# Routing kernel: the second products of 64-row pieces as two column halves side by side

## The chip, the cores and the metric

The kernel runs on one core of one Trainium2 chip. The metric is the device time of one execution in microseconds (us). TensorE does the matrix products, VectorE (DVE), ScalarE (ACT) and GpSimd (POOL) work on elements, SyncE (SP) issues transfers, and each engine works through its own queue in order. Matrix products read SBUF and write PSUM, which has eight banks of 512 float32 per partition here.

## The reference

A decayed linear attention over 8 batches, 8 heads, 576 positions and a head size of 64 gives 4608 rows of 512 values. A router then picks two of eight experts for every row, and each expert is a pair of products with a ReLU between them:

```
logits = x @ w_gate ; noisy = logits + log1p(exp(x @ w_noise)) * noise
top2 = the two largest of noisy ; weights = softmax over these two
for e in range(8):
    for k in range(2):
        mask = top2[:, k] == e
        h = maximum(x[mask] @ w1[e], 0)          # 512 -> 1024
        out[mask] += weight * (h @ w2[e])        # 1024 -> 512
```

## The kernel before

The first 195 us or so hold the attention, the routing and a few early expert tiles. After them the expert tiles follow one another.

**Pieces and tiles.** Each expert has room for 1216 rows: nine pieces of 128 rows and a tenth (number 9) of 64. `tiles()` puts one to four pieces into a tile and sorts the pieces of a tile by size, so a 64-row piece always comes first in its tile. Numbered in order, tiles 0 to 8 are early ones, and tiles 9 to 28 are the wide ones. The 64-row pieces lie in tile 9 (with three full pieces, expert 0), tile 11 (with one, expert 1), tile 13 (with two, expert 2), and tiles 16, 19, 22, 25 and 28 (with one each, experts 3 to 7). Before tiles 16, 19, 22, 25 and 28 lie two tiles of four full pieces each.

**The two products.** `wide()` (line 1050) makes the first product of tile i: for each of eight groups f, four matmuls (line 1063) of 128x128 weights against all the rows of the tile, so 128x512 for a tile of four pieces and 128x192 for a full piece and a 64-row one. The result takes a PSUM buffer `p`, and ACT or DVE applies the ReLU (lines 1046 and 1048) into `hT`, four SBUF buffers that each hold two groups. Between these matmuls lie those of the second product of tile i-1: `down()` (line 1081) cuts its 8 times m matmuls (m pieces) into eight parts of m. `second()` (line 1114) is one of them: 128 columns of `hT` as weights against a 128x512 slice of w2, eight of them accumulating into one PSUM buffer `po` per piece. For a 64-row piece the same 128 columns are loaded, and the lower 64 rows of the result are not used. The pieces come one after the other in the order of the tile.

**What follows a piece.** When the last of its eight matmuls is done, `finish()` (line 1134) reads `po`. Rows whose first choice is this expert are scaled on ACT or DVE (lines 1148 and 1150) and written by SP to a scratch array `yd`. For rows with their second choice here, DVE multiplies and adds the earlier half (line 1158), which POOL has gathered from `yd` (line 1129), and POOL scatters the sum into the output (line 1162). Of the 64-row pieces, the one of expert 0 goes the first way and the other seven go the second way. The second product of tile 28 has no next tile to lie in: it runs at the end, piece by piece, the 64-row piece first.

**Order.** The order of the work on each engine is laid down ahead by a planner (`Plan.run`). It knows an estimated cost for every operation, hands out buffers, and picks the operation that could start soonest. Buffers have quotas: the expert stream holds at most four PSUM buffers at a time while other streams are open, and `half` buffers (which hold `hT`, the gathered halves and the outputs) number 21. For a group, the planner sees one TensorE operation with all its matmuls. The gathers of the rows of later tiles (line 961) are paced: each waits for the last TensorE matmul that was emitted before it (`self.mm`). For a piece in which first and second choices meet, DVE prepares weights and indices from the gathered row (lines 1001 to 1007). In the last wide tile, POOL has a drain (line 1250) in its queue.

Of the kernel before, what the change touches and what calls it, by code (L numbers as in the profile page):

```python
# [21 lines left out]
F = 1024  # L22
DM = 512
KD = DM // P
KF = F // P
# [12 lines left out]
KEY = 8192.0  # L38
NOV = 64
HD = 64  # L40
C9 = 9
NU = 16
MID = 288.0
# [198 lines left out]
class Kernel:  # L242
# [42 lines left out]
    def setup(self):  # L285
# [764 lines left out]
    def wide(self, i, t, prio, g2=None):  # L1050

        pl, nc = self.pl, self.nc
        w, d = self.W[t[0]], self.t[i]
        n, xT, xv = d["w"], d["xT"], d["xv"]
        hT = d["hT"] = [pl.buf("half", "exp") for _ in range(4)]
        for f in range(KF):
            p = self.psum("exp")

            def pe(_, f=f, p=p):
                it = g2(f) if g2 else iter(())  # L1060
                for di in range(KD):
                    o = di * F + f * P
                    self.mm = nc.tensor.matmul(p.t[:, :n], lhsT=w.t[:, o:o + P], rhs=xv()[:, di, :n],  # L1063
                                               start=(di == 0), stop=(di == KD - 1))
                    next(it, None)
                for _ in it:
                    pass
            r, ww, c = [xT] + [(w, k) for k in range(KD)], [p], 0.435 * n / 256
            if g2:
                r2, w2, c2 = g2.deps(f)  # L1070
                r, ww, c = r + r2, ww + w2, c + c2
            pl.op("PE", c, pe, r=r, w=ww, prio=prio)
            hv = lambda f=f: hT[f // 2].t.bitcast(BF16).rearrange("p (f s) -> p f s", f=2)[:, f % 2, :n]
            op = pl.op({"ACT": 0.17 + 0.00084 * n, "DVE": 0.1 + 0.00115 * n}, 0, lambda g, p=p, hv=hv: self.relu(
                g, hv(), p.t[:, :n]), r=[p], w=[(hT[f // 2], f)], prio=prio)
            if g2:
                for s in g2.ends(f):
                    self.finish(i - 1, g2.t, s, prio)
        return op

    def down(self, i, t):

        nc = self.nc
        e, js, _ = t
        w, d = self.W[e], self.t[i]
        po = d["po"] = [self.psum("exp") for _ in js]
        hT, m = d["hT"], len(js)
        part = lambda g: [divmod(x, KF) for x in range(g * m, g * m + m)]

        class Down:  # L1090
            def __call__(_, g):
                for s, f in part(g):
                    self.second(e, po[s], hT, self.off(js)[s], f)
                    yield

            @staticmethod
            def deps(g):
                return ([(hT[f // (KF // len(hT))], f if len(hT) == 4 else f // 2) for s, f in part(g)] +
                        [(w, KD + f // 2) for s, f in part(g)], [po[s] for s in sorted({s for s, f in part(g)})],
                        0.216 * m)  # L1100

            @staticmethod
            def ends(g):
                return [s for s, f in part(g) if f == KF - 1]
        Down.t = t
        return Down()

    def second(self, e, po, hT, c, f):


        k = KF // len(hT)
        hv = hT[f // k].t.bitcast(BF16).rearrange("p (f s) -> p f s", f=k)[:, f % k]
        o = KD * F + f * DM
        self.mm = self.nc.tensor.matmul(po.t, lhsT=hv[:, c:c + P], rhs=self.W[e].t[:, o:o + DM],  # L1114
                                        start=(f == 0), stop=(f == KF - 1))

    def prev(self, i, t, prio):
        pl, nc = self.pl, self.nc
# [15 lines left out]
    def finish(self, i, t, s, prio):  # L1134
        pl, nc, tc = self.pl, self.nc, self.tc
        e, js, _ = t
        d = self.t[i]
        j = js[s]
        k = self.kind(e, j)
        g, io, _, src = d["gi"][s]  # L1140
        src = list(src) if isinstance(src, tuple) else [src]
        po, n = d["po"][s], self.size(j)
        if k != "S":
            y = pl.buf("half", "exp")

            def ev(eng, y=y, po=po, g=g, n=n):
                if eng == "ACT":
                    nc.scalar.activation(y.t[:n], po.t[:n], Act.Copy, scale=g()[:n])  # L1148
                else:
                    nc.vector.tensor_scalar(y.t[:n], po.t[:n], g()[:n], None, Alu.mult)  # L1150
            pl.op({"ACT": 0.69, "DVE": 0.7}, 0, ev, r=[po] + src, w=[y], prio=prio)
            r0 = P + YOFF[e] + j * P
            key = self.ydk.setdefault(e, pl.fix())
            pl.op("SP", 0.07, lambda q, y=y, r0=r0, n=n: nc.sync.dma_start(
                out=self.yd[r0:r0 + n, :], in_=y.t[:n]), r=[y], w=[(key, j)], prio=prio, dma=0.7)
        if k != "F":
            o, b = pl.buf("half", "exp"), d["prv"][s]
            pl.op("DVE", 0.75, lambda _, o=o, b=b, po=po, g=g, n=n: nc.vector.scalar_tensor_tensor(  # L1158
                o.t[:n], po.t[:n], g()[:n], b.t[:n], Alu.mult, Alu.add), r=[po, b] + src, w=[o], prio=prio)

            def scat(_, o=o, io=io, n=n):
                ins = nc.gpsimd.indirect_dma_start(  # L1162
                    out=self.out[:, :], out_offset=IOff(ap=io()[:n], axis=0), in_=o.t[:n, :], in_offset=None,
                    bounds_check=N - 1, oob_is_err=False).ins
# [7 lines left out]
    def record(self):  # L1172
        pl = self.pl
# [7 lines left out]
        for u in range(NU + 1):  # L1181
# [14 lines left out]
            if u and u % 4 == 0:  # L1196
                pr = u - 0.4
# [5 lines left out]
        ts = self.tiles()  # L1203
# [3 lines left out]
        last = {t[0]: i for i, t in enumerate(ts)}  # L1207
# [7 lines left out]
        for i, t in enumerate(ts[:ne]):  # L1215
            pr = 100 + 4 * i
            while fetched < min(ne, i + 3):
                self.fetch(fetched, ts[fetched], 100 + 4 * fetched)
                fetched += 1
            begun = [self.up(i, t, pr)]  # L1220
            g = self.down(i, t)
            for k in range(KF):
                r, w, c = g.deps(k)
                pl.op("PE", c, lambda _, g=g, k=k: [0 for _ in g(k)], r=r, w=w, prio=pr)
                for s in g.ends(k):
                    self.finish(i, t, s, pr)
        prev = None
        for i in range(ne, len(ts) + 1):
            pr = 100 + 4 * i
            while fetched < min(len(ts), i + 1 + ahead):  # L1230
                self.fetch(fetched, ts[fetched], 100 + 4 * fetched - 2)
                fetched += 1
            if i < len(ts):
                e = ts[i][0]
                if i == last[e] and e + 3 < E:
                    self.weights(e + 3, pr, False, begun)
                late = i > ne and ts[i - 1][0] < e and any(self.kind(*x) != "S" for x in self.pieces(ts[i - 1]))
                if not late:
                    self.prev(i, ts[i], pr)
                begun = [self.wide(i, ts[i], pr, prev)]  # L1240
                if late:
                    self.prev(i, ts[i], pr)
            else:
                e, po, hT = ts[-1][0], self.t[i - 1]["po"], self.t[i - 1]["hT"]
                for s in range(len(po)):
                    pl.op("PE", 1.74, lambda _, s=s: [self.second(e, po[s], hT, self.off(ts[-1][1])[s], f) for f in range(KF)],
                          r=[(hT[f // 2], f) for f in range(KF)] + [(self.W[e], KD + f) for f in range(4)], w=[po[s]], prio=pr)
                    self.finish(i - 1, ts[-1], s, pr)
            if i == len(ts) - 1:
                pl.op("POOL", 6.0, lambda _: self.nc.gpsimd.drain(), prio=pr - 6, after=self.scats[i - 2][:1])  # L1250
            if i < len(ts):
                prev = self.down(i, ts[i])
# [159 lines left out]
```

## Time and profile before

| | |
|---|---|
| median of 3 runs | 440.3 us (438.19 to 440.85) |
| profiled execution | 441.0 us, span 439.4 us |
| TensorE busy | 385.7 us (88%) |
| GpSimd busy | 286.3 us (65%) |
| ScalarE busy | 240.0 us (55%) |
| VectorE busy | 179.7 us (41%) |
| mean DMA rate | 240 GB/s |

Line numbers (L1114) are those of the kernel. `PE` is TensorE's matmul row, `PEld` its weight loads. A matmul's record is longer than the distance to the next one, as they are pipelined: what a stream of them takes is read from start to start. Idle time of an engine is put down to what ended it. A few matmul records are missing from a trace.

### The profile page before, as it was taken

To read this page: it belongs to the slowest core of one execution; us is meant where nothing else is said; L and a number is where in the kernel's file an instruction comes from. 1 tells how busy PE (TensorE), PEld (TensorE's weight loads), DVE (VectorE), ACT (ScalarE), POOL (GpSimd) and SP (SyncE) were. 2 spreads that over 40 slices of the span, in tenths; PEclk is the share of its full clock that TensorE was granted. 3 is DMA by queue.
4 is the path that set the end of the run, shared out by engine and by line. 5 is a ranking of instruction groups with operands and counts; after the bars stand their busy time and mean duration, and the time that the engine had idled before them with its cause. 6 is when DMAs were issued, how large, how long until landed. Compare 5 with 4: busy or idle time off the path is not lost. (4 is left out here: it accounts for less than half of the span.)

```text
span 439.4 us, 11080 instructions
## 1 busy us (share of the span) xinstructions
PE 385.7 (88%) x4252; PEld 245.4 (56%) x4288; DVE 179.7 (41%) x489; ACT 240.0 (55%) x398; POOL 286.3 (65%) x355
## 2 busy tenths in 40 slices
PE   1787884889898959899979999999999999999992
PEld 1665774777676746575545545555454454454451
DVE  2544388778378278213043334026025031131221
ACT  3589693866787436466554747446536524424320
POOL 8875678997789337553446566566577677567344
PEclk9999597969899969999999999999999999999998
DMA  7999999999999988448399897895799997645323
GB/s 193 276 309 233 291 240 310 318 212 247 314 263 196 227 168 242 118 137 297 116 325 387 261 382 236 276 383 167 251 352 278 292 212 224 187 157 174 121 78 140
DMA packets 102489, 105.34 MB, mean 240 GB/s; under 512 B 31870, under 2 KB 80511, under 8 KB 102434
## 3 DMA queue, kind: packets, MB, share of 16 engines
q1 hardware_dynamic: 87170, 67.72, 51.3%
q0 software_dynamic: 15264, 36.89, 32.7%
q8 instruction: 34, 0.56, 0.5%
q14 instruction: 21, 0.17, 0.1%
HBM read 83.20 MB, written 26.63 MB: 250 GB/s over the span
## 5 line engine op out<-in xcount | busy, mean ns | idle before, releaser
L1114 PE MATMUL ps<-W,half 128*128 128x512 bf16 x608 | 202.8, 383 | 0.7 <-issue 0.2
L1063 PE MATMUL ps<-big,W 128*128 128x512 bf16 (+4 forms) x636 | 189.0, 330 | 4.0 <-DVE half L1048 2.8
L1046 ACT ACTIVATE half<-ps 128x512 bf16<-128x512 f32 (+5 forms) x179 | 90.2, 506 | 117.6 <-PE ps L1063 100.7
L961 POOL DMA_INDIRECT xg<-xd,xi x80 | 83.1, 1039 | 64.6 <-ACT half L1046 20.5
L1114 PEld LDWEIGHTS <-half 128*128 128x128 bf16 x640 | 62.6, 99 | 72.6 <-issue 5.6
L1063 PEld LDWEIGHTS <-W 128*128 128x128 bf16 x640 | 63.0, 98 | 47.6 <-issue 0.3
L1158 DVE SCALAR_TENSOR_TENSOR half<-ps,xg,half 128x512 f32<-128x512 f32 (+1 forms) x39 | 29.2, 749 | 79.9 <-PE ps L1114 68.6
L1162 POOL DMA_INDIRECT out_dram<-half,xg x39 | 38.8, 995 | 26.3 <-issue 12.5
L515 DVE TENSOR_TENSOR half<-ps,mask 128x512 bf16<-128x512 f32 x64 | 40.0, 683 | 20.2 <-PE ps L507 20.0
L1129 POOL DMA_INDIRECT half<-yd,xg x39 | 39.4, 1011 | 11.9 <-issue 10.4
L276 ACT ACTIVATE half<-ps 128x1024 bf16<-128x1024 bf16 (+1 forms) x33 | 32.7, 1010 | 12.1 <-PE ps L482 9.4
L482 PE MATMUL ps<-ident__69,half 128*128 128x128 bf16 x256 | 23.8, 251 | 16.6 <-ACT half L449 9.1
L457 POOL TENSOR_TENSOR half<-big,tab 128x1024 bf16<-128x1024 f32 x15 | 28.6, 1904 | 10.3 <-DMA big<-in_q_dram 10.3
L1037 PE MATMUL ps<-half,W 128*128 128x256 bf16 (+1 forms) x288 | 29.8, 260 | 4.5 <-ACT half L276 2.8
L464 POOL TENSOR_TENSOR half<-big,tab 128x512 bf16<-128x512 f32 x32 | 33.0, 1046 | 0.0
L1148 ACT ACTIVATE half<-ps,xg 128x512 f32<-128x512 f32 (+1 forms) x32 | 21.8, 685 | 16.1 <-PE ps L1114 15.8
L482 PEld LDWEIGHTS <-half 128*128 128x128 bf16 x256 | 18.6, 114 | 19.5 <-ACT half L449 9.6
L1037 PEld LDWEIGHTS <-W 128*128 128x128 bf16 x288 | 24.6, 100 | 8.2 <-issue 3.8
L276 ACT ACTIVATE tb<-ps 64x512 bf16<-64x512 f32 x32 | 18.9, 590 | 13.5 <-PE ps L540 13.3
L276 ACT ACTIVATE W<-big 128x1024 bf16<-128x1024 f32 x21 | 21.4, 1055 | 5.7 <-DMA big<-in_moe_w_dram 5.5
L276 ACT ACTIVATE xT<-ps 128x512 bf16<-128x512 f32 (+1 forms) x40 | 19.9, 556 | 7.2 <-PE ps L656 5.0
L1158 DVE SCALAR_TENSOR_TENSOR half<-ps,gm,half 128x512 f32<-128x512 f32 x6 | 4.5, 751 | 46.9 <-ACT half L1148 39.8
(170 smaller groups left out, 415.7 us busy)
## 6 DMA issues: line engine op xcount, KB each, us to landing
big<-in_moe_w_dram SPq DMA_DIRECT2D x40, 512.0 KB, 8.9
yd<-half SPq DMA_DIRECT2D x41, 256.0 KB, 5.2
big<-in_k_dram SPq DMA_DIRECT2D x32, 256.0 KB, 6.1
big<-in_q_dram SPq DMA_DIRECT2D x16, 512.0 KB, 6.0
big<-in_v_dram SPq DMA_DIRECT2D x32, 256.0 KB, 6.3
W<-in_moe_w_dram POOLq DMA_DIRECT2D x12, 512.0 KB, 10.5
xd<-xg SPq DMA_DIRECT2D x16, 264.0 KB, 5.0
xg<-xd,xi POOLq DMA_INDIRECT x80, 4.4
```

What stands on the lines that cost most here:

```text
L276: self.nc.scalar.activation(out, in_, Act.Copy)
L464: self.eng(e).tensor_tensor(o, i, t, Alu.mult)
L482: nc.tensor.transpose(v[:, hp, x, :], i[:, y, hp * P:(hp + 1) * P], ident.t)
L515: nc.vector.tensor_tensor(S.t.bitcast(BF16).rearrange("p (h c x) -> p h c x", h=2, c=2)[:, h], p[h].t.rearrange("p (c x) -> p c x", c=2), ...
L961: ins = nc.gpsimd.indirect_dma_start(out=x.t[:n, :], out_offset=None, in_=self.xd[:rows, :], in_offset=IOff(ap=xi.t[:n, h:h + 1], axis=0), ...
L1037: nc.tensor.matmul(pv()[:, f2, :], lhsT=w.t[:, o:o + P], rhs=xv()[:, di, :n], start=(di == 0), stop=(di == KD - 1))
L1046: self.nc.scalar.activation(o, i, Act.Relu)
L1063: self.mm = nc.tensor.matmul(p.t[:, :n], lhsT=w.t[:, o:o + P], rhs=xv()[:, di, :n], start=(di == 0), stop=(di == KD - 1))
L1114: self.mm = self.nc.tensor.matmul(po.t, lhsT=hv[:, c:c + P], rhs=self.W[e].t[:, o:o + DM], start=(f == 0), stop=(f == KF - 1))
L1129: pl.op("POOL", 1.3, lambda _, b=b, iy=iy, n=self.size(j): nc.gpsimd.indirect_dma_start(out=b.t[:n, :], out_offset=None, in_=self.yd[:rows ...
L1158: pl.op("DVE", 0.75, lambda _, o=o, b=b, po=po, g=g, n=n: nc.vector.scalar_tensor_tensor(o.t[:n], po.t[:n], g()[:n], b.t[:n], Alu.mult, Al ...
L1162: ins = nc.gpsimd.indirect_dma_start(out=self.out[:, :], out_offset=IOff(ap=io()[:n], axis=0), in_=o.t[:n, :], in_offset=None, bounds_chec ...
```

## The change

For a 64-row piece, the eight matmuls of the second product become sixteen. Each has 64 columns of `hT` as weights against 256 of the 512 columns of w2: the left half of the result goes to partitions 0 to 63 of the piece's PSUM buffer, the right half to partitions 64 to 127, both in its first 256 elements. So two matmuls with the same weights stand next to each other on the two column halves of the array.

These sixteen no longer lie between the matmuls of the next tile's first product. The eight parts of `down()` are now made of the full pieces only (n of them), and the 64-row piece follows in one block behind the last part. `deps` and `ends` are told so, and the planner's cost of the last part grows by 1.05. In the last tile the 64-row piece stays first, with a cost of 0.95 in place of 1.74.

`finish()` reads such a piece in two instructions of 64x256, one for each half, in place of one of 64x512; the planner's costs for them become 0.86 on ACT and for the multiply-add on DVE, and 0.8 for the scaling on DVE.

```
@@ down
-        part = lambda g: [divmod(x, KF) for x in range(g * m, g * m + m)]
+        full = [s for s in range(m) if self.size(js[s]) == P]
+        short = [s for s in range(m) if self.size(js[s]) < P]
+        n = len(full)
+        part = lambda g: [(full[x // KF], x % KF) for x in range(g * n, g * n + n)]
+        alone = lambda g: [(s, f) for s in short for f in range(KF)] if g == KF - 1 else []
...
+            def rest(g):
+                for s in short if g == KF - 1 else ():
+                    self.halves(e, po[s], hT, self.off(js)[s])
...
+    def halves(self, e, po, hT, c):
+        k = KF // len(hT)
+        for f in range(KF):
+            hv = hT[f // k].t.bitcast(BF16).rearrange("p (f s) -> p f s", f=k)[:, f % k]
+            o = KD * F + f * DM
+            for y in range(2):
+                self.mm = self.nc.tensor.matmul(po.t[y * HD:(y + 1) * HD, :MIDC], lhsT=hv[:, c:c + HD],
+                                                rhs=self.W[e].t[:, o + y * MIDC:o + (y + 1) * MIDC],
+                                                start=(f == 0), stop=(f == KF - 1), skip_group_check=True)
+
+    @staticmethod
+    def sums(po, n):
+        return [(slice(0, DM), po.t[:n])] if n == P else [
+            (slice(y * MIDC, (y + 1) * MIDC), po.t[y * HD:(y + 1) * HD, :MIDC]) for y in range(2)]
@@ wide, behind the last matmul of a group
+                if g2:
+                    g2.rest(f)
@@ finish
-            pl.op("DVE", 0.75, lambda _, o=o, b=b, po=po, g=g, n=n: nc.vector.scalar_tensor_tensor(
-                o.t[:n], po.t[:n], g()[:n], b.t[:n], Alu.mult, Alu.add), r=[po, b] + src, w=[o], prio=prio)
+            pl.op("DVE", 0.75 if n == P else 0.86, lambda _, o=o, b=b, po=po, g=g, n=n: [nc.vector.scalar_tensor_tensor(
+                o.t[:n, c], x, g()[:n], b.t[:n, c], Alu.mult, Alu.add) for c, x in self.sums(po, n)],
+                r=[po, b] + src, w=[o], prio=prio)
```

More of the change, by code (lines that the diff above doesn't have):

```diff
@@ L40 @@
 HD = 64
+MIDC = DM // 2
 C9 = 9
@@ L1223, in record @@
                 r, w, c = g.deps(k)
-                pl.op("PE", c, lambda _, g=g, k=k: [0 for _ in g(k)], r=r, w=w, prio=pr)
+                pl.op("PE", c, lambda _, g=g, k=k: ([0 for _ in g(k)], g.rest(k)), r=r, w=w, prio=pr)
                 for s in g.ends(k):
@@ L1245, in record, with last @@
                 for s in range(len(po)):
-                    pl.op("PE", 1.74, lambda _, s=s: [self.second(e, po[s], hT, self.off(ts[-1][1])[s], f) for f in range(KF)],
+                    def last(_, s=s):
+                        c = self.off(ts[-1][1])[s]
+                        if self.size(ts[-1][1][s]) < P:
+                            self.halves(e, po[s], hT, c)
+                        else:
+                            for f in range(KF):
+                                self.second(e, po[s], hT, c, f)
+                    pl.op("PE", 1.74 if self.size(ts[-1][1][s]) == P else 0.95, last,
                           r=[(hT[f // 2], f) for f in range(KF)] + [(self.W[e], KD + f) for f in range(4)], w=[po[s]], prio=pr)
```

21 lines of the change are left out of this document (12 added, 9 removed).

## Prediction

> **What bounds the kernel now.** I read the page first, then the stretches, then TensorE's waits, then the end.
>
> ```profile
> span 439.4 us, 11080 instructions
> PE 385.7 (88%) x4252; PEld 245.4 (56%) x4288; DVE 179.7 (41%) x489; ACT 240.0 (55%) x398; POOL 286.3 (65%) x355
> ...
> PE   1787884889898959899979999999999999999992
> ```
>
> TensorE is filled from about the middle on, and all the second products of 64-row pieces lie there. The busy time of each engine by stretch, and then all of TensorE's waits behind 195 us, say how full it is:
>
> ```profile
> 234.00:413.00 179.00, 177.95 (x985) 91.44 (x1004) 50.79 (x84) 88.31 (x154) 117.38 (x116) 1.00 0.82 257
> 413.00:440.00 27.00, 18.50 (x104) 9.69 (x104) 6.00 (x8) 5.04 (x12) 10.86 (x11) 0.94 0.28 99
> ...
> PE ps L1063 <- DVE half L1048: 2.8, 1, 2.8
> PE ps L983 <- DMA xg<-xd,xi: 0.6, 1, 0.6
> ```
>
> The columns are span, PE, PEld, DVE, ACT, POOL, granted clock, DMA share, GB/s. From 234 to 413 us TensorE is busy 177.95 of 179.00 us at full clock. The waits are two, both before 234 us. So a matmul less in this stretch is its whole time less, as long as nothing else gets late.
>
> The one large wait stands at 224.7 us, in the first product of tile 11 (timelines of PE and of DVE, then one stretch):
>
> ```profile
> 224.72 0.25 PE L1063 MATMUL ps<-big,W 128*128 128x192 bf16 x1
> 227.79 0.24 PE L1063 MATMUL ps<-big,W 128*128 128x192 bf16 x1 [2.82 <-DVE half L1048]
> ...
> 226.91 0.16 DVE L1001 TENSOR_TENSOR gm<-xg 128x1 f32<-128x1 f32 x1 [4.27 <-DMA xg<-xd,xi]
> ...
> 227.38 0.88 DVE L1048 TENSOR_SCALAR half<-ps 128x192 bf16<-128x192 f32 x3
> ...
> 228.50:232.00 3.50, 3.50 (x16) 1.95 (x14) 2.15 (x5) 1.97 (x3) 0.99 (x1) 0.53 1.05 371
> ```
>
> DVE waits 4.27 us for a gathered row, three ReLUs stand behind it, and TensorE runs out of free PSUM buffers. The clock then falls to 0.53 for 3.5 us, which costs another 1.6 us (3.5 times 0.47). This place costs some 4.6 us, and I use it twice below.
>
> **The end is not TensorE's.** The drain on POOL, POOL's queue after it (first and last of ten back-to-back), and DVE's last two:
>
> ```profile
> L1250 POOLq DRAIN  x1: 8001/8001/8001, 413.1 to 413.1; - x1
> ...
> 421.95 0.98 POOL L1162 DMA_INDIRECT out_dram<-half,xg  x1 [7.67 <-DVE half L1158]
> ...
> 433.57 0.99 POOL L1162 DMA_INDIRECT out_dram<-half,xg  x1 [0.30 <-POOLq L1263]
> ...
> 429.97 0.74 DVE L1158 SCALAR_TENSOR_TENSOR half<-ps,xg,half 64x512 f32<-64x512 f32 x1 [0.97 <-PE ps L1114]
> 431.64 0.75 DVE L1158 SCALAR_TENSOR_TENSOR half<-ps,xg,half 128x512 f32<-128x512 f32 x1 [0.93 <-PE ps L1114]
> ```
>
> POOL drains for 8.0 us from 413.1, and then works off ten issues, one per 1.3 us ((433.57 - 421.95)/9). The last scatter starts at 433.57, while its rows were ready at 432.39 (431.64 + 0.75): POOL is about 1 us behind. So the end hangs on when the drain begins. That is in the first product of tile 27, among the finished pieces of tile 26, which TensorE paces: it moves with all that TensorE saves before, and nothing saved after it counts.
>
> **The change part by part.**
>
> *Removed:* eight matmuls of 128x512 for each 64-row piece. Their distance:
>
> ```profile
> 427.77 3.83 PE L1114 MATMUL ps<-W,half 128*128 128x512 bf16 x17
> ```
>
> Sixteen distances are 3.83 less the 0.38 of one matmul: 0.2156 us each. Eight make **1.725 us** a piece.
>
> *Added:* eight pairs of 64-column matmuls. The trace has such pairs: L540 multiplies 128 rows by 64 columns, in turn into the two partition halves of one PSUM buffer. Four short windows on them, each one timeline, all starting with the same pair:
>
> ```profile
> 60.55 0.27 PE L540 MATMUL ps<-half,half 128*64 128x192 bf16 x2
> ...
> 60.55 0.36 PE L540 MATMUL ps<-half,half 128*64 128x192 bf16 x4
> ...
> 60.55 0.42 PE L540 MATMUL ps<-half,half 128*64 128x192 bf16 x8
> ...
> 60.55 0.50 PE L540 MATMUL ps<-half,half 128*64 128x192 bf16 x10
> ```
>
> Both of the first pair fill one 0.27 us. The second pair, also of 192 columns, ends 0.08 to 0.09 later, two pairs of 64 columns (x8) bring 0.06 more, and the next pair of 192 another 0.08. A *single* matmul of 192 columns would take 0.2156 x 192/512 = 0.081. So two run in the time of one, with the loads of their weights (two per pair) hidden. For 256 columns, 0.2156/2 = 0.108 and 0.083 x 256/192 = 0.111 enclose a pair: I take 0.109, and 0.872 us for eight.
>
> What these rows don't show: L540's moving operand is 64 values repeated three times, the new one is 256 different values for each half. If that stopped the overlap, the pair would take twice 0.109, the upper bound (a rival).
>
> *Added too:* the array changes from 128 columns to 64 and back. The same in the trace, on the way in and back:
>
> ```profile
> 109.40 0.59 PE L1114 MATMUL ps<-W,half 128*128 128x512 bf16 x2
> 109.93 0.27 PE L540 MATMUL ps<-half,half 128*64 128x192 bf16 x2
> ...
> 110.26 0.68 PE L540 MATMUL ps<-half,half 128*64 128x192 bf16 x22
> 110.87 0.39 PE L1114 MATMUL ps<-W,half 128*128 128x512 bf16 x1
> ...
> L540 PE MATMUL ps<-half,half x512: 192/213/369, 12.4 to 137.9; 64*64 64x64 bf16 x85, 128*64 128x192 bf16 x43, 128*64 128x64 bf16 x43
> ```
>
> The second L1114 starts at 109.40 + 0.59 - 0.38 = 109.61, L540 0.32 later: 0.10 over the 0.216 of a normal step. On the way back the last of the 22 starts at 110.26 + 0.68 - 0.19 = 110.75 and L1114 0.12 later, about 0.09 over the 0.03 of such a pair. Another 0.02 goes to the first pair after a change (its loads can't be ahead). Together 0.21.
>
> *Sum for a piece:* 0.872 + 0.21 = 1.08 in place of 1.725: **0.64 us less**. Tiles 9, 11, 13, 16, 19, 22 and 25 lie before the drain: 7 x 0.64 = **4.5 us**. The eighth (tile 28) is behind it and I count nothing; were it to count in full, 5.1.
>
> The Trainium skill speaks against the overlap at one point. Its page "TensorE: Matmul & The Clock Gate" (Part 3, "The mechanism") says that weight loads overlap running matmuls only where the row group differs, and both halves here use all rows; "TensorEngine Tiling (Array Packing)" ("Restrictions") adds that column tiling turns fast weight loads off. By the first page's P/1.2 ns for a load ("LDWEIGHTS"), 64 columns take an estimated 53 ns, two of them unhidden 107 ns, and a piece 1.94 us, 1.5 us slower over seven. The rows of L540 disagree: a pair of 64 columns, loads included, took 0.03 us.
>
> *Reading the piece:* DVE reads seven of the eight, ACT or DVE the first. One read in two halves, by rows of DVE reading PSUM:
>
> ```profile
> L1158 DVE SCALAR_TENSOR_TENSOR half<-ps,xg,half 64x512 f32<-64x512 f32 x7 | 5.2, 742 | 19.1 <-PE ps L1114 19.1
> L1048 DVE TENSOR_SCALAR half<-ps 128x320 bf16<-128x320 f32 x5 | 2.5, 492 | 3.9 <-PE ps L1063 3.9
> L1048 DVE TENSOR_SCALAR half<-ps 128x192 bf16<-128x192 f32 x5 | 1.5, 350 | 0.0
> ```
>
> 256 elements lie midway between 192 and 320: 0.42 us, two of them 0.84 at most, against 0.74. This 0.1 is hidden by DVE's idle time (50.79 busy of 179). Without that cover it would cost 0.7 in all.
>
> *Moved:* the block behind the last part. The piece's read, its `yd` write on SP (first piece) or its scatter on POOL (the others) move from the middle of the next tile to its end, past the scatters of the full pieces; their numbers stay. POOL has 117 of 179 us busy, so a later scatter there is hidden; the gathers behind it go at most one issue (1.3 us) later, and rows are fetched several tiles ahead. `hT` of the tile is held whole until the block is done, four `half` buffers instead of one or two at that point, of 21. Three PSUM buffers of the expert stream's four are then taken at once. Both only press if the planner hands a just-used buffer to the next group: a rival.
>
> **Forecast.** The profiled execution took 441.0 us, its span 439.4 and 1.6 around it. Less 4.5 that is 436.5 (span 434.9). It stands 0.7 above the median of the runs, so against the median: 440.3 - 4.5 = **435.8 us**. One per cent, about what a measurement can tell here, is 4.4 us, so the forecast lies on that bound; its own spread, from 6 pieces counted to 8 and from 0.60 to 0.66 a piece, is 435.0 to 436.7.
>
> **Rivals.**
>
> *The stall at 224.7 goes.* The planner's costs change from tile 9 on, and DVE's order with them. Were the ReLUs put ahead of the wait, or on ACT, 4.6 us go too: 431.2. Against it: the waiting row is paced by TensorE and moves with it.
>
> *One more such stall:* 435.8 + 4.6 = 440.4. *Two more, the slower side:* 445.0. The mechanism is DVE's queue: a wait for a gathered row with ReLUs behind it.
>
> ```profile
> DVE gm L1001 <- DMA xg<-xd,xi: 18.9, 5, 6.7
> ```
>
> DVE waits five times in all, up to 6.7 us, and only one wait reaches TensorE, since elsewhere ACT had the ReLUs. A new plan can put ReLUs behind any of the other four. It decides against the change from the moment that one such wait stops TensorE for about 3 us and drops the clock. For it: the block holds back the gathers that wait for it by up to 1.1 us. Against it: those four waits stop nothing on TensorE now.
>
> *PSUM at the boundary.* If the next group waits for the buffer of the 64-row piece, TensorE idles about 0.2 us (DVE starts that long after the product's slot ends: 431.60 for the last matmul's end, 431.64 for DVE), 0.8 for the read, 0.06 back: 1.06 at each of seven boundaries, so 7 x (1.06 - 0.64) = 2.9 slower, 443.2. Against it: eight buffers exist and the one freed longest ago is taken.
>
> *The halves don't run side by side:* sixteen times 0.109 plus 0.21 is 1.95 a piece, 0.23 more than now, 1.6 over seven: 441.9. Loads that stand bare in front of the pairs would turn the sign too, from 0.08 us a pair on (0.64/8). The rows of L540 speak against both. By the rule of the Trainium skill above ("TensorE: Matmul & The Clock Gate") this would be 441.8.
>
> **How the numbers follow.** Forecast 0.47 (0.28 of it below 435.9, where "faster by over 1%" begins), stall gone 0.14, one more stall 0.10, two more 0.14, PSUM 0.09, not side by side 0.06. Faster by over 1%: 0.28 + 0.14 = 0.42. Slower by over 1% (above 444.7): 0.14. Within: 0.44. The range goes from 431.0 (stall gone) to 443.2 (PSUM) and leaves out the two stalls and little else.
>
> **What will show it.** Pairs of L1114's successor starting within 0.01 us of one another, pairs 0.11 apart, a block of about 1.08 us with its changes; TensorE still without waits at the seven boundaries; the drain beginning near 408.6 in place of 413.1, with ten issues behind it as now. The prediction is wrong if TensorE's waits behind 195 us differ from 3.4 us by more than 1, if the block takes over 1.3 us, or if POOL's drain takes another place in its queue.

## The result, and the profile after

On the chip of the profiles the changed kernel took 437.74 us (median of 20 runs, 432.31 to 447.21), the kernel before 438.97 (20 runs, 436.77 to 441.88). The ratio is 0.9915, with a 95% interval of 0.9889 to 0.9941: some 3.7 us less, in place of the 4.5 that were forecast. That ratio leaves out runs that lie over 1.5% above the fastest of their kernel, and here these are nine of the twenty of the changed kernel and none of before; by all runs the medians are 1.2 us apart (0.3%). The profiled execution is one of the long ones: 442.87 us, span 441.3. The forecast range of 431.0 to 443.2 holds the kernel before as well (438.97), so it says little that the new median lies in it. There are two things to explain: that the five shortest runs (432.31 to 435.03) lie 3.0 to 4.5 us below the five shortest of before (436.77 to 438.02), and that the others spread up to 447.

| | before | after |
|---|---|---|
| median of 20 runs, us | 438.97 | 437.74 |
| lowest to highest, us | 5.1 apart | 14.9 apart |
| profiled execution, its span, us | 441.0, 439.4 | 442.87, 441.3 |
| TensorE busy, us | 385.7 | 380.1 |
| TensorE's waits behind 195 us, by the view of waits | 3.4 | 9.3 |
| start of the drain on POOL | 413.1 | 415.2 |

The head of the page of after, its first lines and the slices of TensorE and of its clock:

```profile
span 441.3 us, 11215 instructions
...
PE 380.1 (86%) x4315; PEld 243.3 (55%) x4352; DVE 182.3 (41%) x498; ACT 238.4 (54%) x397; POOL 285.2 (65%) x355
...
PE   1687884979899868899979999999999995999992
...
PEclk9999687789899989999999999999999997999998
```

TensorE works 5.6 us less, and yet the span is 1.9 longer. The slices show where: one digit in the filled half fell from 9 to 5, in the 34th slice, and the clock falls there too.

**The new products themselves.** First the timeline of TensorE at the block of the first 64-row piece of the expert stage (start, duration, then engine, line, operation), then all records of one line (L1136 is the pair of halves, L1064 the first products, L1126 the full second products, L984 transposes of gathered rows):

```profile
218.16 0.33 PE L1064 MATMUL ps<-big,W 128*128 128x384 bf16 x1
218.41 1.06 PE L1136 MATMUL ps<-W,half 128*64 128x256 bf16 x16
219.41 0.40 PE L984 MATMUL ps<-ident__69,xg 128*128 128x128 bf16 x4
...
L1136 PE MATMUL ps<-W,half x128: 272/273/297, 218.4 to 431.5; 128*64 128x256 bf16 x128
```

Sixteen matmuls of 256 columns end 1.06 us after the first began, and one alone lasts 0.273: fifteen steps in 0.79. By the trace's start stamps the two of a pair start 3 to 4 ns apart and pairs follow each other after 110 ns (134 after the first), the same in all eight blocks. The step in takes 0.25, of which 0.162 is the matmul of 384 columns (0.2156 x 384/512), so the change of the array costs 0.09; the step out takes 0.21 from the last pair's start (219.20 by the stamps), 0.10 over a pair. From the last old start to the next one that is 1.09 us of the block and its changes.

**The new wait.** All waits of TensorE behind 195 us, then ACT's waits of 345 to 413 us (what waited, for what: us in total, times, longest):

```profile
PE ps L1064 <- ACT half L1047: 5.4, 3, 4.7
PE ps L1064 <- DVE half L1049: 3.2, 1, 3.2
PE ps L984 <- DMA xg<-xd,xi: 0.7, 1, 0.7
...
ACT half L1047 <- PE ps L1064: 29.7, 34, 2.0
ACT half L1047 <- DMA out_dram<-half,im: 6.5, 1, 6.5
ACT half L1047 <- DMA yd<-half: 5.9, 1, 5.9
ACT half L1047 <- DMA out_dram<-half,xg: 2.9, 1, 2.9
```

The second and third are the two that stood there before (2.8 and 0.6). The first is new. It comes from ACT, whose ReLUs wait three times for a DMA. In the same stretch of before ACT waits for TensorE and nearly nothing else:

```profile
ACT half L1046 <- PE ps L1063: 38.5, 45, 1.2
ACT half L1046 <- PE ps L1114: 1.4, 2, 0.7
ACT half L1046 <- issue: 0.9, 1, 0.9
```

The timeline of ACT in after says which ReLUs they are, and the stretch around them (span, PE, PEld, DVE, ACT, POOL busy, granted clock, DMA share, GB/s) what it costs:

```profile
360.97 0.55 ACT L1047 ACTIVATE half<-ps 128x192 bf16<-128x192 f32 x2 [6.48 <-DMA out_dram<-half,im]
364.43 1.09 ACT L1047 ACTIVATE half<-ps 128x512 bf16<-128x512 f32 x2 [2.91 <-DMA out_dram<-half,xg]
371.38 2.06 ACT L1047 ACTIVATE half<-ps 128x512 bf16<-128x512 f32 x4 [5.87 <-DMA yd<-half]
...
357.00:375.00 18.00, 12.53 (x61) 5.39 (x61) 2.22 (x4) 4.68 (x10) 8.22 (x9) 0.85 1.08 237
```

They write the fourth part of `hT` of tile 22 and the first two of tile 23, into `half` buffers which a scatter or a `yd` write is still reading. TensorE stops for 4.9 us right behind the block of tile 22 (367.0 to 372.0 by the stamps). From 372 to 380 it is busy again at a granted clock of 0.73 (the view of stretches), which costs another 2.2 us (8 times 0.27). The same stretch of before:

```profile
357.00:375.00 18.00, 17.95 (x91) 8.66 (x91) 2.99 (x4) 7.36 (x15) 13.80 (x14) 1.00 0.88 198
```

TensorE has 5.4 us less work done there, and the DMA engines are full (1.08) where they were at 0.88. The transfers themselves are late too. The view of DMA from 345 to 375, in before and then in after, ends with the median from issue to landing in us:

```profile
yd<-half SPq DMA_DIRECT2D x3, 256.0 KB, 3.4
...
yd<-half SPq DMA_DIRECT2D x3, 256.0 KB, 11.0
```

Transposes (`big<-xg`) go from 4.1 to 8.5 there and gathered rows (`xg<-xd,xi`) from 3.5 to 10.8, though fewer bytes move (6.16 MB in place of 6.78); from 200 to 340 the `yd` writes stand at 7.6 and 7.4. So in this execution the buffers were not only handed out early: what was still reading them also landed late.

**The time by tile.** The records of the weight loads are complete in every trace (640 of the first products, L1063 or L1064, 32 for each of tiles 9 to 28). So the start of the first load of a tile is a mark that can be compared between kernels: load number 0 for tile 9, 96 for tile 12, 416 for tile 22, 480 for 24, 544 for 26. Times between those marks, us, for all profiled executions (the experiments are told below; the last column is the span less the start of tile 9):

| | chip | 12 to 22 | 22 to 24 | 24 to 26 | 26 to end | 9 to 22 | 22 to end | 9 to end |
|---|---|---|---|---|---|---|---|---|
| before | first | 117.50 | 19.9 | 23.4 | 45.3 | 153.6 | 88.6 | 242.2 |
| after | first | 114.89 | 20.5 | 30.1 | 44.0 | 149.1 | 94.6 | 243.7 |
| before (e5) | 7 | 125.17 | 20.3 | 25.8 | 47.9 | 160.8 | 94.0 | 254.7 |
| after (e1) | 7 | 115.14 | 25.2 | 24.0 | 47.9 | 151.1 | 97.1 | 248.1 |
| after (e6) | 7 | 114.89 | 26.8 | 33.1 | 48.3 | 152.3 | 108.2 | 260.4 |
| after (e10) | 15 | 118.57 | 24.2 | 30.8 | 46.5 | 154.6 | 101.5 | 256.1 |
| after (e12) | 15 | 114.89 | 22.3 | 36.5 | 47.1 | 150.7 | 105.9 | 256.6 |
| order alone (e2) | 7 | 122.98 | 27.7 | 23.4 | 47.6 | 157.9 | 98.6 | 256.6 |
| early block (e3) | 7 | 125.15 | 21.9 | 26.0 | 49.2 | 160.9 | 97.1 | 258.0 |
| 23 buffers (e4) | 7 | 116.14 | 24.1 | 39.5 | 47.8 | 151.5 | 111.4 | 263.0 |
| halves, plan of before (e7) | 7 | 121.58 | 27.1 | 23.4 | 49.3 | 156.2 | 99.7 | 255.9 |
| the same (e9) | 15 | 119.95 | 22.4 | 26.3 | 48.6 | 153.3 | 97.3 | 250.6 |
| old products, plan of after (e8) | 7 | 117.50 | 23.8 | 28.9 | 48.9 | 153.4 | 101.5 | 254.9 |
| five ReLUs in spare buffers (e11) | 15 | 116.41 | 24.8 | 33.6 | 47.1 | 152.4 | 105.5 | 258.0 |

Four blocks lie between the starts of tiles 12 and 22, and 117.50 - 114.89 is 2.61: **0.65 us a piece** against the 0.64 forecast. It can be read this cleanly because TensorE never waits there in those executions. By tile 24 the changed kernel is 3.9 us ahead of before (173.51 - 169.65 from tile 9's start). Between 24 and 26 it loses 6.7, which the stop (4.9) and the low clock behind it (2.2) cover. So in this execution the saving was there in full and was given back at one place.

### The profile page after: what moved, and what is told of

It reads as the page before. It is cut to its first block, busy times and chain, and to the rows that moved or that the text cites. A ratio compares the mean times of both kernels' runs of the same rounds, so it can differ in the third digit from the quotient of the medians.

```text
span 441.3 us, 11215 instructions
## 1 busy us (share of the span) xinstructions
PE 380.1 (86%) x4315; PEld 243.3 (55%) x4352; DVE 182.3 (41%) x498; ACT 238.4 (54%) x397; POOL 285.2 (65%) x355
## 5 line engine op out<-in xcount | busy, mean ns | idle before, releaser
L1064 PE MATMUL ps<-big,W 128*128 128x512 bf16 (+4 forms) x631 | 180.2, 330 | 9.5 <-ACT half L1047 5.4
L1126 PE MATMUL ps<-W,half 128*128 128x512 bf16 x548 | 182.3, 384 | 1.5 <-ACT half L1047 0.7
L1047 ACT ACTIVATE half<-ps 128x512 bf16<-128x512 f32 (+5 forms) x179 | 88.8, 504 | 120.3 <-PE ps L1064 89.9
L1126 PEld LDWEIGHTS <-half 128*128 128x128 bf16 x576 | 56.1, 99 | 70.7 <-issue 7.6
L1064 PEld LDWEIGHTS <-W 128*128 128x128 bf16 x640 | 62.8, 98 | 48.3 <-issue 1.9
L1188 DVE SCALAR_TENSOR_TENSOR half<-ps,xg,half 128x512 f32<-128x512 f32 (+1 forms) x46 | 30.5, 667 | 66.5 <-PE ps L1126 48.8
L516 DVE TENSOR_TENSOR half<-ps,mask 128x512 bf16<-128x512 f32 x64 | 39.9, 682 | 22.4 <-PE ps L508 22.2
L1158 POOL DMA_INDIRECT half<-yd,xg x39 | 39.1, 1002 | 11.9 <-issue 9.5
L483 PE MATMUL ps<-ident__69,half 128*128 128x128 bf16 x256 | 24.2, 257 | 18.2 <-POOL half L458 9.1
L1038 PE MATMUL ps<-half,W 128*128 128x256 bf16 (+1 forms) x288 | 28.9, 255 | 5.2 <-ACT half L277 2.6
L483 PEld LDWEIGHTS <-half 128*128 128x128 bf16 x256 | 19.0, 116 | 20.9 <-POOL half L458 10.6
L1178 ACT ACTIVATE half<-ps,xg 128x512 f32<-128x512 f32 x32 | 21.8, 684 | 16.1 <-PE ps L1126 16.0
L1038 PEld LDWEIGHTS <-W 128*128 128x128 bf16 x288 | 23.9, 98 | 8.8 <-issue 3.6
L277 ACT ACTIVATE xT<-ps 128x512 bf16<-128x512 f32 (+1 forms) x40 | 19.9, 558 | 8.3 <-PE ps L657 4.8
```

The source lines that it names most:

```text
L277: self.nc.scalar.activation(out, in_, Act.Copy)
L483: nc.tensor.transpose(v[:, hp, x, :], i[:, y, hp * P:(hp + 1) * P], ident.t)
L516: nc.vector.tensor_tensor(S.t.bitcast(BF16).rearrange("p (h c x) -> p h c x", h=2, c=2)[:, h], p[h].t.rearrange("p (c x) -> p c x", c=2), ...
L1038: nc.tensor.matmul(pv()[:, f2, :], lhsT=w.t[:, o:o + P], rhs=xv()[:, di, :n], start=(di == 0), stop=(di == KD - 1))
L1047: self.nc.scalar.activation(o, i, Act.Relu)
L1158: pl.op("POOL", 1.3, lambda _, b=b, iy=iy, n=self.size(j): nc.gpsimd.indirect_dma_start(out=b.t[:n, :], out_offset=None, in_=self.yd[:rows ...
```

## The experiments

All of them ran on two other chips, here called 7 and 15, on which the kernel before takes about 458 and 461 us, 20 more than on the first. This limits what they can say of the first. The releaser "issue" or "remote" (none that the trace names) is frequent in those traces, which hold fewer semaphore records (about 5,700 against 8,355); the start marks above do not depend on them.

The theories at the outset (the recorded expectations name them buffer or plan theory, and rival): **hold** (the late block holds `hT` whole, and the planner's next buffers are ones still being read), against **transfers** (the landings are what is due last behind tile 22, and whatever TensorE saves only moves the wait).

**The two kernels again: e1, e6, e10, e12 (changed) and e5 (before).** No edit.

> The changed kernel as it is. Buffer theory (the block holds all four hT buffers to the end of the tile, so ReLUs of the next tile get buffers that a scatter still reads, and their wait varies with the landing of DMAs): runs spread over some 10 us or more, from about 432 to 447, median 436 to 438, and the profile shows ReLUs on ACT that wait for a DMA of out_dram or yd. Rival (disturbance of the chip, not of this kernel): a spread of 5 us like the kernel before.

> The changed kernel beside the three others on one chip. Plan theory (the matmuls save 4.5 us, the new plan gives most of it back in waits on DMA landings): within 1% of before, spread wider than that of before. Rival (matmuls save less than counted): waits like before and blocks longer than 1.1 us.

> The changed kernel beside it. Plan theory: where before takes about 439 us, a median 1 to 4 us below it, 1 to 4 us above the halves under the old plan, and a spread of 10 us or more; where before takes about 458, 1 to 5 us above before. Rival: the same time and spread as the halves under the old plan.

> The changed kernel beside it, as the control. Both theories: within 1% of before where before takes about 458 us, with a spread above 8 us.

> The kernel before, to have its profile on the same chip as the others. All theories: the same time as before, within 1%. Chip theory (a chip with slower DMA lets the plan of before stall too): where its time is about 458 us, TensorE's waits behind the start of tile 9 sum to 10 us or more, and to 4 us where its time is about 439.

Measured, medians with their runs: e1 461.31 (453.30 to 464.16, 12 runs) against 458.45 (17 runs), ratio 1.0001 [0.9928, 1.0074]; e6 463.02 (458.01 to 472.70, 10 runs), 1.0053 [1.0007, 1.0099]; e12 463.18 (459.47 to 466.83, 6 runs), 1.0141 [1.0028, 1.0253]; e10 464.33 (453.74 to 467.08, 6 runs), with no ratio. The kernel before against itself, e5: 458.22 (10 runs) against 458.42 (34 runs), ratio 0.9944 [0.9899, 0.9989]. Equal kernels thus came out 0.6% apart, with an interval that leaves out 1: on these chips an interval of this size is too narrow, and I read nothing under 1% as a difference.

So on both chips no gain is seen; by the medians of all runs the change costs 0.5 to 1.0%. Nor do its runs spread more than those of before here (e1 10.9 us against 10.1, e6 14.7 against 12.9), so e1's expectation of a wider spread isn't met. The wait comes back in e6, timeline of ACT:

```profile
373.11 0.55 ACT L1047 ACTIVATE half<-ps 128x192 bf16<-128x192 f32 x2 [10.54 <-DMA out_dram<-half,im]
378.05 1.08 ACT L1047 ACTIVATE half<-ps 128x512 bf16<-128x512 f32 x2 [4.39 <-DMA out_dram<-half,xg]
385.50 3.05 ACT L1047 ACTIVATE half<-ps 128x512 bf16<-128x512 f32 x6 [6.37 <-DMA yd<-half]
```

The same three ReLUs wait for the same three transfers. But not in every execution of this kernel. In e12 the first and the third wait (7.55 us, releaser not named, and 4.24), in e10 only the second (4.04), and in e1 none of them waits for a transfer; two lines of its timeline of ACT hold all three:

```profile
371.78 0.78 ACT L1047 ACTIVATE half<-ps 128x192 bf16<-128x192 f32 x3 [4.02 <-PE ps L1126]
373.34 1.57 ACT L1047 ACTIVATE half<-ps 128x512 bf16<-128x512 f32 x3 [0.78 <-DVE half L1188]
```

e1 is a short run (453.92 us) and e6 a longer one (464.56) of the same kernel, with the same order of instructions, on one chip. Their spans differ by 10.7 us, and so do their times from tile 22 to 26 (49.2 and 59.9 by the table): in this pair the whole difference arises there. e1 isn't free of loss either: it needs 25.2 from 22 to 24, where e5 needs 20.3, with a wait of 5.05 us of an earlier ReLU for an unnamed releaser. In the table the changed kernel needs 114.9 to 118.6 us from tile 12 to 22 on these chips, up to 10 less than before in e5 (125.17), and then 97 to 108 from tile 22 to the end where e5 needs 94.

**e2, the order alone.** The products of the 64-row piece stand behind the full ones, but as the old eight of 512 columns; the result is the same.

```diff
-                    self.halves(e, po[s], hT, self.off(js)[s])
+                    for f in range(KF):
+                        self.second(e, po[s], hT, self.off(js)[s], f)
...
-                        0.216 * n + (1.05 if alone(g) else 0.0))
+                        0.216 * n + (1.74 if alone(g) else 0.0))
...
```

> The 64-row pieces keep their eight 128x512 matmuls and their single read, and only move behind the full pieces of the tile. Buffer theory: the hold is there and no time is saved, so 439 to 446 us, slower than before by 1 to 5 us in the median, with a spread of 8 us or more. Rival (the column halves themselves, their switches or their two reads bring the new waits): 438 to 440, spread under 6 us, no ReLU waits for a DMA.

Measured: 462.58 (461.06 to 465.60, 4 runs), ratio 1.0161 [1.0083, 1.0239]: 4.1 us above before by the medians, as the buffer theory has it, with a spread of 4.5 in place of 8. With another cost it also gets another plan, so this is the order with a plan of its own. The stretch of 24 to 26, where the changed kernel loses, is undisturbed here (23.4, as in before on the first chip); 12 to 22 (122.98, where 117.50 is the time without waits) and 22 to 24 (27.7) are long instead. In this plan the loss lies at other places.

**e3, the block early.** The halves stand behind the second group instead of the last, so that `hT` of the tile isn't held whole.

```diff
-        alone = lambda g: [(s, f) for s in short for f in range(KF)] if g == KF - 1 else []
+        alone = lambda g: [(s, f) for s in short for f in range(KF)] if g == 1 else []
...
```

> The block of column halves stands behind the second part instead of the last, so the full pieces release hT one buffer after the other as before. Buffer theory: the 7 x 0.64 us are saved and nothing is lost: 433.5 to 435.5 us, spread under 6 us, no ReLU waits for a scatter. Rival (any new plan of the order brings such waits): like the changed kernel, median 436 to 438 with a spread of 10 us.

Measured: 463.48 (460.78 to 465.82, 6 runs), ratio 1.0164 [1.0101, 1.0227]. The buffer theory's 433.5 to 435.5, 4 us under before, has failed: without the late hold the time is no better. But this plan is another one too, with its own waits: 12 to 22 takes 125.15. So the late hold of `hT` alone isn't what the time on this chip hangs on.

**e4, two more `half` buffers**, 23 in place of 21:

```diff
-        pl.cls("half", mk("half", 21, [P, 512], F32), cs=9, exp=15, xt=3, tl=6, rt=1)
+        pl.cls("half", mk("half", 23, [P, 512], F32), cs=9, exp=15, xt=3, tl=6, rt=1)
```

> The changed kernel with 23 half buffers in place of 21 (all that fit). Buffer theory: the waits of ReLUs for scatters shrink or go, median 433.5 to 436, spread under 8 us. Rival (order of gathers and scatters on GpSimd, not the number of buffers): median 436 to 438 and a spread of 10 us or more as in the changed kernel.

Measured: 464.21 (459.80 to 471.77, 5 runs), ratio 1.0112 [1.0026, 1.0199]. This misses the buffer theory's gain too. ACT's waits of 345 to 420 us in e4's profiled run, the longest of the five, still hold these:

```profile
ACT half L1047 <- DMA yd<-half: 9.5, 1, 9.5
...
ACT half L1047 <- DMA out_dram<-half,xg: 2.7, 1, 2.7
```

With two more buffers one under transfer is still handed out. This speaks against a plain shortage of buffers, but not yet against the wait as the cause.

**e8, the plan of the changed kernel with the old products.** Order, costs, buffers and queues as in after; only the sixteen halves are eight matmuls of 512 columns again, read in one piece.

```diff
-                    self.halves(e, po[s], hT, self.off(js)[s])
+                    for f in range(KF):
+                        self.second(e, po[s], hT, self.off(js)[s], f)
...
-        return [(slice(0, DM), po.t[:n])] if n == P else [
+        return [(slice(0, DM), po.t[:n])] if n <= P else [
...
```

> Plan alone: the planner is told the changed kernel (costs, order and buffers of it), but the 64-row pieces run their eight 128x512 matmuls and the single read, at the place of the block. Plan theory: above before by 2 to 5 us and above the changed kernel by 1 to 4.5 us, spread over 8 us. Rival (the new order costs nothing, the halves do): the same as before within 1 us.

Measured: 460.31 (454.60 to 465.60, 10 runs), ratio 1.0005 [0.9942, 1.0069]; e6, run alongside it, is at 463.02. The plan theory of this experiment has failed: it had the old products 2 to 5 us above before and 1 to 4.5 above the changed kernel, and they came out 1.9 above before by the medians, level with it by the ratio, and 2.7 below the changed kernel. What the rival said, that the new order alone costs nothing, fits the ratio. This is the one comparison in which only the products and their read differ. From tile 12 to 22 they bring 117.50 - 114.89 = 2.61 us, in e8 and e6 as on the first chip. From there to the end e8 took 101.5 and e6 108.2. And the same ReLUs wait in e8, timeline of ACT:

```profile
373.31 0.55 ACT L1047 ACTIVATE half<-ps 128x192 bf16<-128x192 f32 x2 [5.66 <-DMA out_dram<-half,im]
377.32 1.08 ACT L1047 ACTIVATE half<-ps 128x512 bf16<-128x512 f32 x2 [3.46 <-issue]
382.59 3.04 ACT L1047 ACTIVATE half<-ps 128x512 bf16<-128x512 f32 x6 [4.18 <-DMA yd<-half]
```

The first ReLU goes on at 373.31 in e8 and at 373.11 in e6, from starts of tile 9 at 204.0 and 202.6. Its wait is 5.66 in the one and 10.54 in the other. So the wait comes with the plan, not with the halves. That a faster TensorE merely comes earlier to the same transfer, and so waits longer, fits this pair of executions; it isn't shown, since e1, the changed kernel with the same saving, has no such wait.

**e7 and e9, the plan of before with the halves.** Costs, buffers and order as in before; the block of halves stands at the group where the piece's last product stood. e7 on chip 7, e9 on chip 15.

```diff
+                    if self.size(js[s]) < P:
+                        continue
...
+                for s, f in part(g):
+                    if self.size(js[s]) < P and f == KF - 1:
+                        self.halves(e, po[s], hT, self.off(js)[s])
...
```

> Halves alone: the planner is told the kernel before, costs, order and buffers unchanged, and only the matmuls issued differ: nothing for the 64-row piece in its parts, and the block of column halves at the end of the group in which its last matmul lay; its read is in two halves. Plan theory: the full 7 x 0.64 = 4.5 us below before (ratio 0.990 at 440 us), spread as before. Rival (any saving on TensorE is eaten by the DMAs and GpSimd behind it): within 1.5 us of before, with waits grown by 3 us or more.

> Halves alone under the plan of the kernel before, once more. Plan theory: where the kernel before takes about 439 us, 4.5 us below it (ratio 0.990) with a spread of at most 6 us and TensorE's waits behind the start of tile 9 at 3 to 5 us; where the kernel before takes about 458 (its waits are 10 us or more there), within 1% of it. Rival (the saving is eaten everywhere by transfers): within 0.5% of before on either.

Measured: e7 461.17 (456.57 to 463.18, 12 runs), ratio 1.0032 [0.9992, 1.0072]; e9 459.51 (454.68 to 463.55, 12 runs), 1.0006 [0.9956, 1.0055]. Had the 4.5 us been kept, the ratio would be 0.990. Neither interval holds that, though e5 has shown that an interval can be off by some 0.5%; so a full saving isn't seen here either, with another plan and other waits. That speaks against the planner's choice of buffers as the sole cause: e7 meets its rival (within 1.5 us by the ratio, TensorE's waits behind 195 us at 15.4 in place of e5's 9.8), and e9 meets both of its theories and decides nothing. TensorE's largest waits in e9 behind 195 us:

```profile
PE ps L1064 <- issue: 5.7, 4, 2.3
PE ps L1125 <- issue: 2.8, 3, 2.2
PE ps L1125 <- ACT half L1047: 2.5, 1, 2.5
PE ps L984 <- DMA xg<-xd,xi: 0.8, 1, 0.8
```

and in before on chip 7 (e5):

```profile
PE ps L1114 <- issue: 4.8, 4, 3.8
PE ps L1063 <- issue: 4.1, 5, 2.1
PE ps L983 <- DMA xg<-xd,xi: 0.9, 1, 0.9
```

Before itself waits 9.8 us there, against 3.4 on the first chip: here the part behind tile 9 isn't TensorE's alone even without the change.

**e11, the waiting ReLUs in spare buffers.** The plan of after to the last instruction; only five outputs of ReLUs (the fourth part of `hT` of tile 22, three of tile 23, one of tile 24) go to buffers of the attention stage, idle by then, so that these ReLUs wait for no transfer.

```diff
+        def swap():
+            for (i, k), s in zip(((22, 3), (23, 0), (23, 1), (23, 2), (24, 0)), K.pl.slots["tb"]):
+                K.t[i]["hT"][k].t = s[2].rearrange("p y n d -> p (y n d)").bitcast(F32)
...
```

> The changed kernel with its order and buffers, except that five ReLU outputs (tile 22's fourth hT buffer, tile 23's first three, tile 24's first) go to five buffers of the attention stage that are idle by then, so that these ReLUs wait for no DMA. Plan theory (the planner's choice of buffers there gives the saved time back): the three waits of ACT on out_dram and yd at tiles 22 and 23 are gone, TensorE's waits there (5 to 9 us in the changed kernel) fall under 2, and the median lies 3 to 8 us below the changed kernel's on the same chip. Rival (the transfers bind there, the buffers only show it): the waits turn up in another place and the median is within 1.5 us of the changed kernel's.

Measured: 462.74 (453.85 to 467.18, 12 runs) against 460.71 (17 runs), ratio 1.0046 [0.9966, 1.0125]; e12, the changed kernel as it is and run alongside it, has 463.18. The three waits are gone, but the 3 to 8 us that the plan theory forecast aren't gained: by the medians of all runs it is 0.4 us, by the two ratios to before (1.0046 and e12's 1.0141, with intervals that overlap) 1% at most. What waits in e11 is shown by the waits of TensorE behind 195 us (first two rows), then those of ACT and of DVE from 345 to 420:

```profile
PE ps L1127 <- issue: 3.5, 6, 0.9
PE ps L1127 <- DVE half L1189: 3.5, 1, 3.5
...
ACT half L1048 <- remote: 10.4, 2, 6.0
...
DVE half L1189 <- DMA half<-yd,xg: 14.5, 4, 8.0
...
DVE half L1189 <- DMA half<-yd,im: 7.6, 1, 7.6
DVE half L1189 <- DMA out_dram<-half,xg: 5.0, 1, 5.0
```

L1189 adds a piece's product to the row gathered from `yd`. It waits 22 us in all for those gathered rows (14.5 + 7.6), and TensorE waits once behind it for PSUM (3.5). Such waits of DVE aren't new, though: e6 has 21.6 us for gathered rows from 345 to 420 and after 11.9. New are two ReLUs of a later tile, at 401 and 407 us, that wait 10.4 us for a releaser that the trace doesn't name; in e6, e10 and e12 these two don't wait. They lie in the stretch of 24 to 26, which takes 33.6 here and 36.5 in e12. So **these five buffers fall as the cause** of the whole loss on chip 15: with them free, ReLUs wait at a later place and the time is nearly the same. That the transfers are what is due last there fits e7 and e11. It isn't shown by an experiment that speeds a transfer up, the unnamed releaser could be a buffer once more, and on the first chip e11 wasn't run.

## Why the prediction was right, and where it was not

*TensorE bounds the middle, so a matmul less is its whole time less.* Right up to tile 22: 2.61 us for four pieces where nothing waits, and the 114.89 us of the changed kernel came out the same in one execution on each of the three chips. The clause "as long as nothing else gets late" is the one that failed, from tile 22 on.

*The pair takes 0.109, the change of the array 0.21 in all, a piece 1.08 in place of 1.725.* Right: 0.110, 0.09 in, 0.10 out and 0.024 at the first pair; 0.65 saved a piece against 0.64. The way back hit by luck in part: the last of the 22 matmuls ahead of L1114 were 64*64 ones (the row of L540 lists them, the merged line shows only its first form), so it was read on another change of the array than the one that was added. The halves ran side by side though their moving operand differs. The rule of the Trainium skill that was set against it ("TensorE: Matmul & The Clock Gate", Part 3, "The mechanism": loads overlap only where the row group differs) does not hold in this trace: by it the block would be 1.5 us slower over seven pieces, and the pairs follow after 0.110 us with two loads each. As the same section of the Trainium skill also lets a load go ahead into a background weight buffer, only the short rule is contradicted by this trace.

*The reads cost nothing.* Right. DVE's last two reads, where they stand closest to the end (timeline of DVE in after):

```profile
431.91 0.98 DVE L1188 SCALAR_TENSOR_TENSOR half<-ps,xg,half 64x256 f32<-64x256 f32 x2 [0.25 <-PE ps L1136]
433.68 0.75 DVE L1188 SCALAR_TENSOR_TENSOR half<-ps,xg,half 128x512 f32<-128x512 f32 x1 [0.80 <-PE ps L1126]
```

Two halves take 0.98, not 0.84, and DVE still waits for TensorE behind them.

*The end is POOL's, and the eighth piece doesn't count.* Right. The drain and the last of the issues behind it:

```profile
L1288 POOLq DRAIN  x1: 7999/7999/7999, 415.2 to 415.2; - x1
...
424.05 0.98 POOL L1193 DMA_INDIRECT out_dram<-half,xg  x1 [7.64 <-issue]
...
435.67 0.99 POOL L1193 DMA_INDIRECT out_dram<-half,xg  x1 [0.30 <-POOLq L1301]
```

The last rows were ready at 434.43 (433.68 + 0.75), and POOL comes to them 1.24 later, as it was about 1 late before. Ten issues behind a drain of 8.0 us, 1.29 apart. The drain started at 415.2 and not near 408.6, since the new wait lies ahead of it.

*TensorE's waits behind 195 us stay within 1 of 3.4.* Wrong in the profiled execution: 9.3. This was named as what would make the prediction wrong, and by it the prediction's mechanism is wrong for such executions. The step that failed is "*Moved*", in the sentence that `hT` held whole and PSUM held at once "only press if the planner hands a just-used buffer to the next group". The planner did that, but with `half` buffers, which the rival left out; I had priced PSUM alone (1.06 a boundary), and TensorE never waited at a boundary for the halves' reads; at the one boundary where it stopped (367.0) it waited for ReLUs that were late. The price of one such wait was near the rival "one more such stall" (4.6 expected; 6.7 lost between tiles 24 and 26, stop and clock together), with ACT and a buffer's readers in place of DVE and a gathered row.

*The stall at 224.7.* It stayed (3.36 us by the stamps, 2.98 before), as the forecast assumed; the drop of the clock behind it, 1.6 us, did not come in that execution. That adds up: six blocks at 0.64 make 3.84, plus 1.6, less 0.4 for the longer stall and 1.0 for two short waits ahead of tile 24, is 4.0, and 3.9 was measured at tile 24.

*The time.* The forecast of 435.8 was 1.9 below the median, which is inside the range. By the medians of all runs 1.2 us were saved, about a quarter of the 4.5. The likely reading is that short runs keep the saving (before's 438.97 less 4.5 is 434.5; the shortest five lie at 432.3 to 435.0) and that the wait pulls the others up. On that chip this rests on one profiled execution, a long one; the pair e1 and e6 shows such a difference on another chip. So the number fits in part by luck: the median lies between runs that keep the saving and runs with a wait that the forecast put at nothing.

*Left open.* Why the same order of instructions has the wait in some executions and not in others, and so whether the choice of buffers or the late transfers is the cause. How much of the saving the plan of before would keep with the halves on the first chip (e7 and e9 ran elsewhere). What e11's five buffers would gain on the first chip. What makes chips 7 and 15 some 20 us slower for every kernel. None of the versions tried beats both kernels.

## What to carry to other kernels

A saving on the engine that bounds a stretch is worth its size only up to the next point where something paced by another thing meets it: in the profiled execution it was whole for 13 tiles and gone in the next four, so compare two traces by marks of equal work, tile by tile, and not by their ends. A block of work that is moved holds its inputs and shifts its outputs, and a planner then hands out other buffers; before costing that at nothing, list which buffers the next group is given and which transfer still reads them. Look at the spread and at a second chip as well as at the median: by the medians of all runs the same change was 0.3% faster on one chip and 0.5 to 1.0% slower on two others.

## What the runs showed of the hardware

- The kernel before took 439 us on one chip and 458 to 461 on two others (medians). TensorE's pace isn't the difference: where nothing waits, 12 to 22 takes the same 117.50 us (old products, e8) or 114.89 (new, e6 and e12) there as on the first chip. The longer time is spread over the stages: in e5 the span is 18.3 us longer, of which 5.8 lie ahead of tile 9, 7.2 between 9 and 22, 5.3 from 22 on.
- Two matmuls on the two column halves, all 128 rows each, start 3 to 4 ns apart in after, and pairs follow every 110 ns with two loads of 64 columns each; half a 512-column matmul's distance is 108.
- The change between 128 and 64 columns costs 0.09 to 0.10 us each way, in seven of after's eight blocks on the way in and in seven on the way out (the eighth way out is the stop at 367, the eighth way in stands behind a matmul whose record is missing).
- The kernel before against itself on one chip gave a ratio of 0.9944 with an interval of 0.9899 to 0.9989. Such an interval is no proof of a difference below 1%.
